# Two megabytes of weight loads under way in place of one, from the fourth pair on, in a fused attention and expert kernel

## The chip, the cores and the metric

The kernel runs on one core of a Trainium2 chip. The metric is the device time of one execution in microseconds (us), lower is better. The core has five engines with an instruction queue each: TensorE (PE; its loading of stationary operands is shown as PEld), VectorE (DVE), ScalarE (ACT), GpSimd (POOL) and SyncE (SP), which here issues nearly all DMA transfers. Each queue runs in its own order; between queues, semaphores decide.

## What is computed

A linear attention with decay over 2 x 8 heads, 768 positions in blocks of 64, then two dense layers with a leaky ReLU between, then two more with a softmax-like gate and a normalisation. The attention output, turned to 1536 tokens x 512, is the input of the rest. The weights are 64-bit floats in memory.

```python
for b in range(nb):                       # 12 blocks of 64 positions
    intra = einsum('bhic,bhjc->bhij', qb, kb) * Dmask
    intra = einsum('bhij,bhjd->bhid', intra, vb)
    inter = einsum('bhid,bhde->bhie', qb * lam_pow, kv_state)
    out[:, :, sl] = intra + inter
    kv_state = lam_block * kv_state + einsum('bhsd,bhse->bhde', kb * rev_pow, vb)
h = x @ w_in                              # 1536x512 @ 512x2048
x = maximum(0.01 * h, h) @ w_out          # 2048x512
h = x @ w_in2                             # 512x1024
solu = h * softmax(h)
ln = (solu - mean) / sqrt(var + 1e-06) * g_ln
return ln @ w_out2                        # 1024x512
```

## The kernel before

The weights of the first two layers come in 17 pairs, counted from 0. Pair n has two halves of 128 x 1024 32-bit words (512 KB): block n of w_in and block n-1 of w_out (pair 0 has the first only, pair 16 the second only). `load_weights(n)` issues the halves from SP. A pair is then turned from 64-bit floats into two matmul operands, a high and a low piece: ACT reads both words (`words`, that is L350 and L354), DVE clamps, shifts and joins them (L360, L370, L379), ACT copies the high piece (`high`, L409), DVE subtracts it for the low piece (`low`, L428). Each pair must have landed before ACT's L350 of it.

The main loop runs over 48 items (3 blocks of 512 tokens, 16 blocks of the hidden layer). For item i, PE runs `l1_mm` of the item (12 matmuls, L439, into one of two `hps` banks), at some items a `step` of the attention (the chunks from 4 on, 8 of them), and `l2_mm` of the item before (12 matmuls, L456, into `acc`). ACT and DVE make the input of `l2_mm` in `l1_split`: prelu (L442) and `ghi` (L445) on ACT, `glo` (L447) on DVE. While the first 16 items run, the pairs are converted ahead of them: at item i, `high` and `low` of pair i+1, the clamp, shift and join of pair i+2, `words` of pair i+3, and `load_weights` of pair i+5. The order on each engine is the order in which the code is written; an instruction that waits holds up all behind it. In ACT's queue, `words` of pair i+3 stands ahead of `high` and of `l1_split` of the next item. At a step, DVE also evicts the scores (`scores_ev`, L204), which frees the `hps` bank for the item after.

All loads go through `load` (L113 to L125). It keeps a list of the loads so far with their sizes, adds up sizes from the newest back, and where the sum with the new load goes over `limit`, the new load waits for that older load to land. `AHEAD` is 2 MB (4 halves, the new one counted), `CALM` is 1 MB (2 halves). The four chunks of attention that are loaded first, the small loads and the later chunks (`load_qk`, `load_kv`, `fix`) have the default `AHEAD`; the weights of L332 have `CALM`, the second half of pair 1 half of it, and pair 0 `AHEAD`. After pair 7, SP issues kv (four loads of 128 KB), `fix` (68 KB) and qk (512 KB), and then pair 8. From chunk 4 on, a kv load also waits until PE and ACT have read the kv of the chunk before, since there is one buffer. `load_weights` of kind "b" (w_out2) uses the same line.

Of the kernel before, what the change touches and what calls it, by code (L numbers as in the profile page):

```python
# [10 lines left out]
U32 = mybir.dt.uint32  # L11
# [13 lines left out]
AHEAD, CALM = 1 << 21, 1 << 20  # L25
# [3 lines left out]
NF = FF1 // P  # L29
# [15 lines left out]
def fused_kernel(ctx: ExitStack, tc: tile.TileContext, att, vt, tab, cst, w_in, w_out, w_in2, w_out2, out):  # L45
# [7 lines left out]
    pe, dve, act, pool, sync = nc.tensor, nc.vector, nc.scalar, nc.gpsimd, nc.sync  # L53
# [59 lines left out]
    def load(queue, out, in_, limit=AHEAD):  # L113

        size = 4
        for n in out.shape:
            size *= n
        ins = queue.dma_start(out=out, in_=in_).ins
        ahead = size
        for before, n in reversed(flight):  # L120
            ahead += n
            if ahead > limit:
                tc.add_manual_dep(ins, before.name, SYNC, reason="bytes under way")
                break
        flight.append((ins, size))  # L125
# [186 lines left out]
    def whole(n):  # L312

        return IN if n == 0 else OUT if n == NF else BOTH

    def load_weights(n, halves=None):
        if n >= len(order):
            return
        kind, f = order[n]
        if n not in raws:  # L320
            if n == NF:
                raws[n] = tmp.tile([P, 1, 512, 2], U32, tag="s", name="rawl")
            else:
                raws[n] = wp.tile([P, 2, 512, 2], U32, tag="w", name="raww")
        t = raws[n]
        if kind == "a":
            load(sync, out=t.rearrange("p h a b -> p (h a b)"), in_=w_in2[f].bitcast(U32))
            return
        halves = halves or whole(n)
        for i in range(halves.start, halves.stop):  # L330
            src = w_out2[f + i] if kind == "b" else w_out[f - 1] if i else w_in[f]
            load(sync, out=t[:, 0 if n == NF else i].rearrange("p a b -> p (a b)"), in_=src.bitcast(U32), limit=(CALM // 2 if n == 1 and i else CALM) if n else AHEAD)  # L332

    def of(n, halves):

# [262 lines left out]
    scan(dfirst, 0, None)  # L598
    load_step(0)
    load_weights(0)  # L600
    load_step(1)
    load_step(2)
    load_step(3)
    load_weights(1, IN)
    load_weights(1, OUT)
    load_weights(2)
    load_weights(3)
# [264 lines left out]
```

## Time and profile before

| | us |
|---|---|
| median of 3 runs | 447.06 (445.94 to 447.09) |
| the profiled execution | 445.46 |
| its span, first to last instruction | 443.70 |
| PE busy | 98% of the span |
| DVE busy | 60% |
| ACT busy | 44% |
| granted clock of TensorE | 1.00 throughout |

In the 40 slices of the page, PE is at nine tenths or more nearly everywhere. DVE is as full from about 10 to 110 us, while the pairs are converted, and the DMA engines move 230 to 300 GB/s in that time and little later. The rows that matter stand further down. In a timeline row, the first number is the start, the second the time until the end of the last of the merged instructions, and the bracket at the end says how long the engine had idled before it and what ended that. A row of a DMA issue gives the size and the time from issue to landing.

### The profile page before, as it was taken

Reading aid. Unit: us, or ns where it says so; the run is one execution under the profiler, and the core shown is the slowest. Engines: PE = TensorE matmul, PEld = TensorE weight load, DVE = VectorE, ACT = ScalarE, POOL = GpSimd, SP = SyncE. Lnnn points to the kernel's source line nnn. Section 1 sums busy time; section 2 is a strip of 40 time slices with the busy share of each in tenths; the row PEclk is TensorE's granted clock in tenths of the full one; section 3 lists DMA queues with packets and bytes.
Section 4 is the critical chain, followed back from the end, with each engine's and each line's share of the span. In section 5 each row is a group of like instructions: output and inputs, shape, how many; then the busy total and the mean of one; then the engine's idle time right before and its main releaser. Section 6 shows DMA issues by size and latency. Waiting matters only on the chain.

```text
span 443.7 us, 8024 instructions
## 1 busy us (share of the span) xinstructions
PE 433.7 (98%) x3270; PEld 356.8 (80%) x3272; DVE 267.3 (60%) x423; ACT 195.6 (44%) x332; POOL 32.0 (7%) x38
## 2 busy tenths in 40 slices
PE   8899998999999999999999999999999999999996
PEld 4788777888888888888888888888888888888886
DVE  4898989999541121211133889716779877777640
ACT  4587866977443222222234778512424322222221
POOL 1500102102201020100000000000000000000000
PEclk9999999999999999999999999999999999999999
DMA  8678788883302030100025542000112222222111
GB/s 296 231 255 260 243 246 236 252 235 98 97 11 87 0 98 0 49 1 0 1 95 188 191 189 96 1 1 10 38 37 72 88 75 73 75 72 74 58 47 47
DMA packets 23699, 46.85 MB, mean 106 GB/s; under 512 B 4336, under 2 KB 12016, under 8 KB 23152
## 3 DMA queue, kind: packets, MB, share of 16 engines
q1 hardware_dynamic: 21792, 44.78, 31.4%
q10 hardware_dynamic: 1872, 1.58, 1.3%
q8 instruction: 25, 0.41, 0.4%
q14 instruction: 10, 0.08, 0.1%
HBM read 37.95 MB, written 3.15 MB: 93 GB/s over the span
## 4 chain that ended last, share of the span: by engine, by line
PE 83%; ACT 0%; issue 0%; DVE 0%
PE acc L456 25%; PE hps L439 25%; PE acc L568 15%; PE aps L476 6%; PE hps L476 5%; PE acc L476 4%; PE aps L250 1%; PE aps L264 1%; PE hps L196 0%; PE aps L210 0%; PE aps L536 0%; PE acc L536 0%; ACT osb L571 0%; DVE state L225 0%
## 5 line engine op out<-in xcount | busy, mean ns | idle before, releaser
L439 PE MATMUL hps<-xhi,wio 128*128 128x512 f32 x384 | 102.9, 390 | 2.7 <-DVE r L204 1.2
L447 DVE TENSOR_TENSOR glo<-hps,ghi 128x512 fp32r<-128x512 f32 x48 | 33.1, 689 | 110.9 <-ACT ghi L445 110.7
L456 PE MATMUL acc<-ghi,wio 128*128 128x512 f32 x384 | 96.1, 392 | 0.6 <-ACT ghi L445 0.6
L439 PEld LDWEIGHTS hps<-xhi,wio 128*128 128x128 f32 x384 | 71.8, 188 | 18.3 <-ACT raww L354 1.6
L456 PEld LDWEIGHTS acc<-ghi,wio 128*128 128x128 f32 x384 | 71.4, 188 | 16.1 <-ACT ghi L445 1.0
L442 ACT ACTIVATE hps<-hps 128x512 f32<-128x512 f32 x48 | 28.0, 584 | 104.9 <-PE hps L439 104.9
L568 PE MATMUL acc<-wb,ln 128*128 128x512 f32 (+1 forms) x312 | 67.6, 373 | 0.0
L568 PEld LDWEIGHTS acc<-wb,ln 128*128 128x128 f32 x312 | 55.3, 188 | 10.2
L439 PE MATMUL hps<-xlo,wio 128*128 128x512 f32 x192 | 51.3, 389 | 0.0
L456 PE MATMUL acc<-glo,wio 128*128 128x512 f32 x192 | 51.3, 389 | 0.0
L439 PEld LDWEIGHTS hps<-xlo,wio 128*128 128x128 f32 x192 | 36.0, 188 | 7.5
L456 PEld LDWEIGHTS acc<-glo,wio 128*128 128x128 f32 x192 | 36.0, 188 | 7.5
L350 ACT ACTIVATE x<-raww 128x1024 f32<-128x1024 f32 (+1 forms) x28 | 27.8, 995 | 11.7 <-DMA raww<-in_w_in_dram 6.6
L379 DVE SCALAR_TENSOR_TENSOR x<-x,raww 128x1024 uint32<-128x1024 uint32 (+1 forms) x28 | 32.2, 1152 | 0.1
L370 DVE SCALAR_TENSOR_TENSOR raww<-x,raww 128x1024 uint32<-128x1024 uint32 (+1 forms) x28 | 29.6, 1056 | 3.8 <-ACT raww L354 1.7
L445 ACT CAST ghi<-hps 128x512 fp32r<-128x512 f32 x48 | 28.2, 587 | 1.5
L354 ACT ACTIVATE raww<-raww 128x1024 uint32<-128x1024 uint16 (+1 forms) x28 | 27.9, 998 | 0.0
L509 POOL TENSOR_TENSOR small<-small,nhalf 128x1 f32<-128x1 f32 x12 | 6.6, 549 | 234.5 <-DVE small L508 234.5
L428 DVE TENSOR_TENSOR wio<-x,wio 128x1024 fp32r<-128x1024 f32 (+1 forms) x21 | 22.2, 1057 | 1.5 <-ACT wio L409 1.5
L409 ACT CAST wio<-x 128x1024 fp32r<-128x1024 f32 (+1 forms) x21 | 17.8, 849 | 11.2 <-DVE x L379 11.2
L165 POOL TENSOR_TENSOR qk<-qk,qpow 128x512 f32<-128x512 f32 x8 | 11.6, 1445 | 140.4 <-PE hps L196 109.6
L571 ACT COPY osb<-acc 128x512 f32<-128x512 f32 (+1 forms) x13 | 7.2, 555 | 32.3 <-PE acc L568 19.5
(115 smaller groups left out, 494.6 us busy)
## 6 DMA issues: line engine op xcount, KB each, us to landing
raww<-in_w_out_dram SPq DMA_DIRECT2D x23, 512.0 KB, 4.3
raww<-in_w_in_dram SPq DMA_DIRECT2D x16, 512.0 KB, 4.3
qk<-in_att_dram SPq DMA_DIRECT2D x8, 512.0 KB, 4.6
raww<-in_w_in_dram SPq DMA_DIRECT2D x4, 1024.0 KB, 4.8
lt<-e SPq DMA_DIRECT2D x124, 32.0 KB, 1.8
out_dram<-osb SPq DMA_DIRECT2D x11, 256.0 KB, 2.2
ldw<-in_att_dram SPq DMA_DIRECT2D x7, 384.0 KB, 5.4
kv<-in_att_dram SPq DMA_DIRECT2D x16, 128.0 KB, 3.4
```

Of the source, the lines that this page charges most:

```text
L350: act.activation(x, raw[:, :, 1].bitcast(F32), AF.Copy, scale=HI_SCALE)
L354: act.activation(raw[:, :, 0], raw.bitcast(U16)[:, :, 1], AF.Copy, scale=LO_SCALE)
L370: dve.scalar_tensor_tensor(raw[:, :, 0], x.bitcast(U32), 3, raw[:, :, 0], op0=ALU.logical_shift_left, op1=ALU.bitwise_or)
L379: dve.scalar_tensor_tensor(xu, xu, 0x80000000, raw[:, :, 0], op0=ALU.bitwise_and, op1=ALU.bitwise_or)
L428: dve.tensor_tensor(t[:, 1, halves], x[:, halves], t[:, 0, halves].bitcast(F32), op=ALU.subtract)
L439: pe.matmul(bank, w[:, s, k], x[b][:, k], start=(i == 0), stop=(i == len(terms) - 1))
L442: act.activation(bank, bank, AF.Prelu, alpha=0.01)
L445: act.copy(ghi, bank)
L447: dve.tensor_tensor(glo, bank, ghi.bitcast(F32), op=ALU.subtract)
L456: pe.matmul(acc[m], w[:, s, m], g, start=(f == 0 and first), stop=(f == NF - 1 and last))
L476: pe.matmul(bank, x[b][:, k, o : o + P], w2_t["a", k, half][:, s], start=(i == 0), stop=(i == len(terms) - 1),)
L568: pe.matmul(po[:, 0:n], x[:, k], w2_t["b", k][:, s, cols], start=(i == 0), stop=(i == len(terms) - 1))
```

## The change

One line in `load_weights`: the limit of a half is 1 MB only for the pairs 1 and 2; from pair 3 on, and for the w_out2 loads, it is 2 MB. Pair 1's second half keeps 0.5 MB, pair 0 keeps 2 MB.

```diff
-load(sync, out=..., in_=src.bitcast(U32), limit=(CALM // 2 if n == 1 and i else CALM) if n else AHEAD)
+load(sync, out=..., in_=src.bitcast(U32), limit=CALM // 2 if n == 1 and i else CALM if n in (1, 2) else AHEAD)
```

The instructions of PE, DVE, ACT and POOL stand in the same order with the same waits. Only what SP's loads wait for differs. Each load counts up one of eight semaphores DMAHW0 to DMAHW7 in turn, and a load that follows 8 loads later on the same one also waits for it. At the first place, the second half of pair 2 counts up DMAHW1, and its first half DMAHW0; the halves of pair 3 count up DMAHW2 and DMAHW3, and qk DMAHW4.

SP, from the second half of pair 2 to pair 4, before:

```order
L118 DMA raww<-in_w_out_dram 128x1024 [waits DMAHW7_49,DMAHW1_49]
L118 DMA raww<-in_w_in_dram 128x1024 [waits DMAHW2_49,DMAHW0_49]
L118 DMA raww<-in_w_out_dram 128x1024 [waits DMAHW3_49,DMAHW1_49]
L118 DMA qk<-in_att_dram 128x2x512
L118 DMA raww<-in_w_in_dram 128x1024 [waits DMAHW5_49,DMAHW3_49]
L118 DMA raww<-in_w_out_dram 128x1024 [waits DMAHW4_49]
```

The same rows of SP after the change:

```order
L118 DMA raww<-in_w_out_dram 128x1024 [waits DMAHW7_49,DMAHW1_49]
L118 DMA raww<-in_w_in_dram 128x1024 [waits DMAHW2_49]
L118 DMA raww<-in_w_out_dram 128x1024 [waits DMAHW3_49]
L118 DMA qk<-in_att_dram 128x2x512 [waits DMAHW0_49]
L118 DMA raww<-in_w_in_dram 128x1024 [waits DMAHW5_49,DMAHW1_49]
L118 DMA raww<-in_w_out_dram 128x1024 [waits DMAHW2_49]
```

The halves of pair 3 no longer wait for pair 2; qk waits for the first half of pair 2, and pair 4 for the second half of pair 2 and the first of pair 3, which are the fourth load before each.

SP, from the second half of pair 7 over kv, `fix` and qk to pair 8, before (`fix` counts up DMAHW1, qk DMAHW2):

```order
L118 DMA raww<-in_w_out_dram 128x1024 [waits DMAHW2_49]
L118 DMA kv<-in_att_dram 64x2x256 x2
L118 DMA kv<-in_vt_dram 64x512 x2
L118 DMA fix<-in_cst_dram 128x136
L118 DMA qk<-in_att_dram 128x2x512 [waits DMAHW3_49]
L118 DMA raww<-in_w_in_dram 128x1024 [waits PE_49,DMAHW1_49,Activation_49,Pool_49]
L118 DMA raww<-in_w_out_dram 128x1024 [waits DMAHW4_49,DMAHW2_49]
```

The same after the change (the second half of pair 7 counts up DMAHW4, the first kv load DMAHW5):

```order
L118 DMA raww<-in_w_out_dram 128x1024 [waits DMAHW0_49]
L118 DMA kv<-in_att_dram 64x2x256 [waits DMAHW1_49]
L118 DMA kv<-in_att_dram 64x2x256
L118 DMA kv<-in_vt_dram 64x512 x2
L118 DMA fix<-in_cst_dram 128x136 [waits DMAHW2_49]
L118 DMA qk<-in_att_dram 128x2x512 [waits DMAHW3_49]
L118 DMA raww<-in_w_in_dram 128x1024 [waits PE_49,DMAHW4_49,Activation_49,Pool_49]
L118 DMA raww<-in_w_out_dram 128x1024 [waits DMAHW5_49]
```

Pair 8 no longer waits for `fix` and qk to land but for the second half of pair 7 and the first kv load; kv and `fix` in turn now wait for halves of pair 6.

## Rows read from the trace of the kernel before

**Rows 1.** The page, busy us of each engine, share of the span, instructions.

```profile
PE 433.7 (98%) x3270; PEld 356.8 (80%) x3272; DVE 267.3 (60%) x423; ACT 195.6 (44%) x332; POOL 32.0 (7%) x38
```

**Rows 2.** Busy time by stretch: us, PE, PEld, DVE, ACT, POOL, PEclk, DMA share, GB/s.

```profile
23.20:45.30 22.10, 22.05 (x96) 17.94 (x96) 20.12 (x35) 18.70 (x32) 0.00 (x0) 1.00 0.78 248
45.30:71.30 26.00, 23.20 (x244) 18.45 (x245) 23.76 (x27) 20.91 (x28) 3.76 (x2) 1.00 0.82 245
71.30:440.30 369.00, 368.98 (x2420) 306.63 (x2420) 208.69 (x334) 144.38 (x245) 20.75 (x24) 1.00 0.25 78
```

**Rows 3.** Timeline of PE, 45.5 to 72.2 us: start, us, instruction, idle before it.

```profile
45.83 0.97 PE L456 MATMUL acc<-ghi,wio 128*128 128x512 f32 x3 [0.56 <-ACT ghi L445]
...
62.06 1.19 PE L439 MATMUL hps<-xhi,wio 128*128 128x512 f32 x4 [1.03 <-ACT wio L409]
...
71.30 1.15 PE L439 MATMUL hps<-xhi,wio 128*128 128x512 f32 x4 [1.25 <-DVE r L204]
```

**Rows 4.** Timeline of ACT, 41 to 62 us.

```profile
41.99 1.14 ACT L350 ACTIVATE x<-raww 128x1024 f32<-128x1024 f32 x1 [0.99 <-DMA raww<-in_w_out_dram]
...
45.19 0.58 ACT L445 CAST ghi<-hps 128x512 fp32r<-128x512 f32 x1
...
54.88 0.59 ACT L445 CAST ghi<-hps 128x512 fp32r<-128x512 f32 x1
58.92 1.12 ACT L350 ACTIVATE x<-raww 128x1024 f32<-128x1024 f32 x1 [3.45 <-DMA raww<-in_w_out_dram]
...
60.97 1.04 ACT L409 CAST wio<-x 128x1024 fp32r<-128x1024 f32 x1
```

**Rows 5.** Waits of DVE, 20 to 72 us: us in total, times, longest.

```profile
DVE x L360 <- ACT x L350: 2.0, 2, 1.5
DVE raww L370 <- ACT raww L354: 0.9, 3, 0.3
```

**Rows 6.** Timeline of DVE, 60 to 71 us.

```profile
60.08 0.69 DVE L360 TENSOR_SCALAR x<-x 128x1024 f32<-128x1024 f32 x1 [1.47 <-ACT x L350]
...
62.25 1.22 DVE L428 TENSOR_TENSOR wio<-x,wio 128x1024 fp32r<-128x1024 f32 x1
...
67.64 2.31 DVE L428 TENSOR_TENSOR wio<-x,wio 128x1024 fp32r<-128x1024 f32 x1
...
70.48 0.67 DVE L204 TENSOR_TENSOR r<-hps,dmask 128x512 f32<-128x512 f32 x1
```

**Rows 7.** Timeline of SP, second halves of the pairs 2, 5 and 8.

```profile
23.22 0.33 SPq L118 DMA_DIRECT2D raww<-in_w_out_dram  x1
...
37.59 0.33 SPq L118 DMA_DIRECT2D raww<-in_w_out_dram  x1
...
54.59 0.33 SPq L118 DMA_DIRECT2D raww<-in_w_out_dram  x1
```

**Rows 8.** Waits of SP, 53 to 60 us: total, times, longest.

```profile
SPq L118 <- DMA fix<-in_cst_dram: 2.7, 1, 2.7
```

**Rows 9.** DMA issues at 23.22, 37.59, 54.59, 75.35 us: KB, us to landing.

```profile
raww<-in_w_out_dram SPq DMA_DIRECT2D x1, 512.0 KB, 3.9
...
raww<-in_w_out_dram SPq DMA_DIRECT2D x1, 512.0 KB, 4.4
...
raww<-in_w_out_dram SPq DMA_DIRECT2D x1, 512.0 KB, 4.3
...
raww<-in_w_in_dram SPq DMA_DIRECT2D x1, 512.0 KB, 3.3
```

**Rows 10.** Busy time by stretch as in rows 2: loads under 2 MB, under 1 MB.

```profile
4.00:16.00 12.00, 11.14 (x307) 7.86 (x310) 7.99 (x21) 5.11 (x13) 4.22 (x4) 1.00 0.94 356
24.00:68.00 44.00, 42.42 (x330) 34.35 (x329) 39.78 (x56) 35.80 (x55) 2.88 (x2) 1.00 0.80 244
```

**Rows 11.** Groups of DVE by form: busy us, mean ns, idle before.

```profile
L204 DVE TENSOR_TENSOR r<-acc,dfirst 128x512 f32<-128x512 f32 x4 | 2.8, 688 | 2.5 <-PE acc L196 2.5
L204 DVE TENSOR_TENSOR r<-hps,dmask 128x512 f32<-128x512 f32 x7 | 4.8, 688 | 0.7 <-PE hps L196 0.6
```

More of the change, by code (lines that the diff above doesn't have):

```diff
@@ L331, in load_weights @@
             src = w_out2[f + i] if kind == "b" else w_out[f - 1] if i else w_in[f]
-            load(sync, out=t[:, 0 if n == NF else i].rearrange("p a b -> p (a b)"), in_=src.bitcast(U32), limit=(CALM // 2 if n == 1 and i else CALM) if n else AHEAD)
+            load(sync, out=t[:, 0 if n == NF else i].rearrange("p a b -> p (a b)"), in_=src.bitcast(U32), limit=CALM // 2 if n == 1 and i else CALM if n in (1, 2) else AHEAD)
     def of(n, halves):
```

## The prediction

> **What bounds the kernel now.** I read the busy times first, then the idle time before TensorE's (PE's) rows in the timeline, then what each of those three waits hangs on, upstream, and last the queue that issues the loads. PE is busy for 433.7 of 443.7 us [rows 1], so a change can win only where PE still idles. From 71.30 to 440.30 us it is busy 368.98 of 369.00 us; from 23.20 to 45.30 us, 22.05 of 22.10; between them, from 45.30 to 71.30 us, 23.20 of 26.00 [rows 2]. Those 2.80 us are three waits in front of PE's rows: 0.56 us at 45.83 for ScalarE's (ACT's) ghi, 1.03 us at 62.06 for ACT's first piece of a weight pair, 1.25 us at 71.30 for VectorE's (DVE's) L204 [rows 3]. Summed, 2.84 us. Since nothing idles behind 71.30, the end moves by what these three lose, and by no more.
>
> All three lead back to loads. Pairs are counted from 0 as in the code; pair n is the half from w_in and the half from w_out.
>
> First wait: ACT idles 0.99 us until 41.99 for the second half of pair 5 [rows 4], which was issued at 37.59 [rows 7] and took 4.4 us to land [rows 9]: 41.99. Behind that wait in ACT's queue stand the two word readings of pair 5 and the high piece of a half of pair 4, and then the prelu and ghi for which PE waits; that ghi ends at 45.78 [rows 4].
>
> Second wait: ACT idles 3.45 us until 58.92 for pair 8 [rows 4], issued at 54.59 [rows 7], landed 4.3 us later [rows 9]. The high piece of pair 7, which PE wants, stands behind it and ends at 62.01.
>
> Third wait: DVE idles 1.47 us until 60.08 for the same reading of pair 8, and from there runs almost without a gap to the L204 that ends at 71.15 [rows 6]. So this wait too is pair 8's landing, passed on through DVE's row.
>
> Pair 8 is late because SP kept it back: SP waited 2.7 us for the small `fix` load before it [rows 8], since with 1 MB allowed the loads ahead of it had to land first.
>
> **The change, part by part.** It adds no instruction to any compute engine and moves none; it changes which landing a load waits for. Three costs follow.
>
> *Rate of the loads.* From 24 to 68 us, with 1 MB allowed, 244 GB/s were moved at a DMA share of 0.80. From 4 to 16 us, where the attention loads already run with 2 MB, it is 356 GB/s at 0.94 [rows 10]. A load that is alone lands in 3.3 us, one of two under way in 4.4 [rows 9], so at 1 MB the engines stand idle part of the time. For the weights at 2 MB the trace has no row; the bounds are 244 (nothing gained) and 356. I take 356, because that row has the same limit and the same queue; its loads have 384 and 256 KB instead of 512, which should not be in its favour.
>
> *When the pairs land.* Up to pair 2's second half, issued at 23.22 and landed 3.9 us later [rows 7, 9], at 27.1, nothing changes. From there, 7 loads of 512 KB (pairs 3 to 5 and one qk) are due up to pair 5: 3.67 MB, 10.3 us at 356 GB/s, so it lands at 37.4 in place of 41.99. Up to pair 8 it is 15 times 512 KB (pairs 3 to 8, two qk, four kv of 128 KB) and 0.07 MB of fix, 7.93 MB: 22.3 us, so 49.4 in place of 58.92. As a test of this sum, at 244 GB/s it gives 27.1 + 32.5 = 59.6, near the 58.92 that the trace has.
>
> *Buffers.* Pairs 6 to 9 take over tiles of the first four attention chunks, all read before the weights' matmuls begin, and pairs 10 and 11 those of pairs 1 and 3, converted long before their turn comes; so no buffer holds these loads. The next load that one holds is kv of step 5, which waits for PE's step 4 before and after alike; SP now stands there longer, with the pairs 12 and on behind it. That costs nothing: they are released after the same step, and with pairs 8 to 11 already landed they no longer wait for them.
>
> Now the three waits. **First:** without ACT's 0.99 us the ghi ends at 44.79, and PE is ready for it at 45.83 − 0.56 = 45.27: gone, 0.48 us to spare. **Second:** PE, 0.56 us earlier, wants the piece of pair 7 at 62.06 − 1.03 − 0.56 = 60.47. ACT is free at 55.47, the end of the ghi at 54.88 [rows 4]; 3.45 us off its end at 62.01 would be 58.56. It also needs DVE's join of pair 7, which was done by 60.08 − 1.47 = 58.61; with 1.04 us for the piece itself, 59.65 at the latest. Gone. **Third:** PE, now 2.84 us earlier, wants DVE's L204 done by 71.15 − 2.84 = 68.31. From 20 to 72 us DVE waits 2.0 + 0.9 us for ACT's word readings (L350, L354) [rows 5], and nearly all of it when ACT itself came late from a load. Given back, the L204 ends at 68.25, just in time. A reserve stands beside it: the L428 at 67.64 took 2.31 us next to GpSimd's scaling; the one at 62.25 took 1.22 [rows 6], and PE's earlier step moves that scaling against DVE's row. So I count the whole 1.25.
>
> After 71.30 both DVE and PE are earlier by the same 2.8 to 2.9 us, so they stand to each other as before, where PE did not wait again. The loads of the last weights also get 2 MB; PE's 368.98 of 369.00 us hide them in either case.
>
> Sum: 0.56 + 1.03 + 1.25 = 2.84 us. The profiled execution took 445.46 us, of which 443.70 are the span; so 442.62 by its own time. It lies 1.60 us under the median of the three runs, 447.06, so **444.2 us** (−0.64%) is forecast there. A measurement of this kernel tells about 0.3%, or 1.3 us, from no change.
>
> How fast must the loads be? The third wait needs pair 8 earlier by 2.9 us, at 56.0: 7.93 MB in 28.9 us, 274 GB/s. Under that the gain shrinks with the landing.
>
> **Rivals.** *1: more loads under way, but hardly more bytes a second.* Then pair 8 comes little earlier and DVE's row carries that on to PE. For it speaks that the 356 GB/s were moved before the weights' matmuls began and by other shapes; against it the DMA share, 0.80 where 0.94 was reached [rows 10]. Halfway between 244 and the 274 that are needed, at 259 GB/s, pair 8 lands at 27.1 + 30.6 = 57.7, 1.2 us earlier, and 445.8 us result; at 244 it is 447.1. A rule speaks for this rival: the Trainium skill, SBUF — State Buffer, section "Can I just issue two DMAs to hit both halves?", says that transfers issued side by side run on the same 16 engines, and that two at once measured only 6% above one. By that rule the rate would rise from 244 to about 259 GB/s, an estimate from it, and the time would be this rival's. The trace has not yet agreed or disagreed for the weights; at its start, with 2 MB, 356 GB/s speak against the rule.
>
> *2: DVE does not get its time back.* DVE is busy 23.76 of 26.00 us in the stretch of the waits [rows 2]; if its 2.9 us stay for other reasons (ACT late for its own work, GpSimd's scaling beside other instructions), the third wait stays and 0.56 + 1.03 = 1.59 us are won: 445.5.
>
> *3: slower, since heavier traffic stretches DVE's instructions.* DVE's row is nearly full from 24 to 68 us, 39.78 of 44.00 [rows 10]. Its 2.9 us of gaps would have to be used up and 1.3 us more, 4.2 of 39.78, so it decides from a stretch of 11%; at 15% (6.0 us) the time would be 450.2. Against it: an L204 of the same size took 688 ns on average, both among the chunks loaded with 2 MB and later [rows 11].
>
> *4: the change does not reach the waits.* If semaphores or buffers hold the loads and not the limit, 447.1. Against it: before pair 8 SP waited for the landing of a load that no buffer needs [rows 8], and the changed program waits there for older ones.
>
> **How the numbers follow.** Forecast 0.72; rival 1 0.12; rival 2 0.08; rival 3 0.05; rival 4 0.03. Rival 2 lies at the edge of what can be told, so 0.05 of it goes to faster and 0.03 to the same: faster 0.77, same 0.12 + 0.03 + 0.03 = 0.18, slower 0.05. The range reaches from 443.4 (the sum and 0.8 us that the three runs lie apart) to 446.0, which takes in rival 2 and the better half of rival 1; left out are rivals 3 and 4 and the rest of 1, some 0.14, and a little noise.
>
> **What would show it.** Right: between 24 and 50 us clearly over 274 GB/s, and then a stretch with hardly a load; pair 8 landed near 49 us; no idle before ACT's L350 for a load past 41 us; none before PE's rows near 45, 60 and 68 us; PE's seamless run from about 68.5 us. Wrong in the first step if the loads stay near 244 GB/s; in the third wait if PE idles at about 68.5 us for DVE with ACT in time; in the sign if DVE's instructions are longer than in the rows here.

## The result and the profile after

The changed kernel takes 441.82 us (441.67 to 442.88), the kernel before 447.07 beside it: a ratio of 0.9893, 95% interval 0.9870 to 0.9915. That is 5.25 us less where 2.84 were forecast, and below the range of 443.4 to 446.0. The profiled execution took 441.67 us, its span 439.9.

Busy time by stretch, answering to [rows 2] (us, PE, PEld, DVE, ACT, POOL, PEclk, DMA share, GB/s):

```profile
23.20:45.30 22.10, 22.10 (x98) 18.30 (x99) 20.76 (x36) 19.84 (x33) 0.00 (x0) 1.00 0.93 330
45.30:71.30 26.00, 26.00 (x261) 21.40 (x260) 25.54 (x32) 20.68 (x28) 5.18 (x3) 1.00 0.66 230
71.30:440.30 369.00, 365.17 (x2405) 303.43 (x2403) 204.71 (x327) 143.85 (x246) 19.71 (x23) 1.00 0.22 73
```

PE idles no more between 45.30 and 71.30 us; the third row ends behind this shorter execution. The chain that ended last now runs through PE alone here; the three blocks that were late in [rows 3]:

```profile
45.13 2.72 PE acc L456 x12
...
60.04 2.72 PE hps L439 x12
...
67.73 2.72 PE hps L439 x12
```

The timeline of ACT, answering to [rows 4]: the reading of pair 5, the ghi behind it, the reading of pair 8 and the high piece of pair 7. None waits for a load.

```profile
40.76 1.14 ACT L350 ACTIVATE x<-raww 128x1024 f32<-128x1024 f32 x1
...
43.98 0.59 ACT L445 CAST ghi<-hps 128x512 fp32r<-128x512 f32 x1
...
54.22 1.18 ACT L350 ACTIVATE x<-raww 128x1024 f32<-128x1024 f32 x1
...
57.49 1.06 ACT L409 CAST wio<-x 128x1024 fp32r<-128x1024 f32 x1 [1.07 <-DVE x L379]
```

DVE's waits from 20 to 72 us, answering to [rows 5], and its timeline, answering to [rows 6]:

```profile
DVE wio L428 <- ACT wio L409: 0.4, 1, 0.4
DVE xlo L303 <- ACT xhi L299: 0.2, 1, 0.2
```

```profile
57.38 0.69 DVE L360 TENSOR_SCALAR x<-x 128x1024 f32<-128x1024 f32 x1
...
64.68 1.22 DVE L428 TENSOR_TENSOR wio<-x,wio 128x1024 fp32r<-128x1024 f32 x1
...
66.42 0.68 DVE L204 TENSOR_TENSOR r<-hps,dmask 128x512 f32<-128x512 f32 x1
```

GpSimd's scaling of `qk` that stands beside the L428, before and after:

```profile
67.24 1.64 POOL L165 TENSOR_TENSOR qk<-qk,qpow 128x512 f32<-128x512 f32 x1 [15.10 <-PE hps L196]
```

```profile
64.92 2.14 POOL L165 TENSOR_TENSOR qk<-qk,qpow 128x512 f32<-128x512 f32 x1 [13.93 <-PE hps L196]
```

SP's issue of the second halves of the pairs 5 and 8, answering to [rows 7], and their landings (KB, us), answering to [rows 9]:

```profile
32.11 0.33 SPq L118 DMA_DIRECT2D raww<-in_w_out_dram  x1
...
44.37 0.41 SPq L118 DMA_DIRECT2D raww<-in_w_out_dram  x1
```

```profile
raww<-in_w_out_dram SPq DMA_DIRECT2D x1, 512.0 KB, 5.0
...
raww<-in_w_out_dram SPq DMA_DIRECT2D x1, 512.0 KB, 6.1
```

So pair 5 landed at 37.1 and pair 8 at 50.5, where 37.4 and 49.4 were worked out. A single load takes longer than before, 6.1 us in place of 4.3, and yet each comes far earlier. The stretch from 24 to 56 us as in [rows 10], and DVE's L204 as in [rows 11]:

```profile
24.00:56.00 32.00, 32.00 (x169) 26.35 (x168) 30.57 (x46) 28.41 (x43) 1.97 (x1) 1.00 0.97 344
```

```profile
L204 DVE TENSOR_TENSOR r<-hps,dmask 128x512 f32<-128x512 f32 x7 | 4.8, 688 | 0.7 <-PE hps L196 0.6
```

344 GB/s at a DMA share of 0.97, and DVE's instruction is as long as before.

The spans of the two profiled executions differ by 443.7 − 439.9 = 3.8 us. The timeline gives 2.84 us of idle time. The rows shown say where most of the rest lies. From the row behind the first wait to the row behind the second it is 16.23 us before and 14.91 after, 1.32 less where 1.03 us of idle time is shown; from there to the row behind the third, 9.24 and 7.69, 1.55 less where 1.25 is shown. Only 0.13 us lie ahead of the weight matmuls, which begin at 23.09 in place of 23.22. What a pause costs beside its idle time, and the 1.5 us by which the medians lie further apart than the profiles, were the questions for the experiments.

### The profile page after: what moved, and what is told of

The parts are those of the page before. It is cut to its first block, busy times and chain, and to the rows that moved or that the text cites. A ratio compares the mean times of both kernels' runs of the same rounds, so it can differ in the third digit from the quotient of the medians.

```text
span 439.9 us, 8018 instructions
## 1 busy us (share of the span) xinstructions
PE 433.0 (98%) x3270; PEld 357.0 (81%) x3272; DVE 266.0 (60%) x423; ACT 195.8 (45%) x332; POOL 32.4 (7%) x38
## 4 chain that ended last, share of the span: by engine, by line
PE 97%; DMA 2%; issue 1%; ACT 0%
PE acc L456 30%; PE hps L439 30%; PE acc L568 15%; PE aps L476 6%; PE hps L476 5%; PE acc L476 4%; PE aps L250 2%; PE aps L264 1%; DMA ldw<-in_att_dram 1%; PE acc L196 1%; DMA tabs<-in_tab_dram 1%; PE aps L210 1%; PE acc L264 1%; PE acc L250 0%; PE aps L582 0%
## 5 line engine op out<-in xcount | busy, mean ns | idle before, releaser
L428 DVE TENSOR_TENSOR wio<-x,wio 128x1024 fp32r<-128x1024 f32 (+1 forms) x21 | 21.1, 1003 | 1.6 <-ACT wio L409 1.5
L571 ACT COPY osb<-acc 128x512 f32<-128x512 f32 (+1 forms) x13 | 7.2, 553 | 32.0 <-PE acc L568 19.5
```

The costliest lines, as they stand in the source:

```text
L428: dve.tensor_tensor(t[:, 1, halves], x[:, halves], t[:, 0, halves].bitcast(F32), op=ALU.subtract)
```

## The experiments

Two theories. **A:** the three waits are all there is, but they cost more than the idle time that one profile showed, since their length changes from execution to execution and each pause costs something besides. **B:** some of the gain lies elsewhere, in the start, in the late loads, or in a rate that helps in another way. All edits are to the limit in `load_weights`, shown as the difference to the changed kernel, but for the pauses.

**The kernel before, profiled once more** (before_again).

```diff
-limit=CALM // 2 if n == 1 and i else CALM if n in (1, 2) else AHEAD
+limit=CALM // 2 if n == 1 and i else CALM if n else AHEAD
```

> The kernel before once more, for a second profiled execution. The changed kernel gained 5.25 us by the medians, but the profiled executions lie only 3.8 us apart, and the profile of before lay 1.6 us under its own median. Theory A (before's loads leave PE waits whose length changes from execution to execution): the three waits of PE between 45 and 72 us stand again, with another sum; an execution near 447 us shows 1 to 1.5 us more of idle time before PE's rows there than the 2.84 us of the first profile. Theory B (the rest of the gain lies elsewhere, at the start or the end): the waits sum to 2.8 us again and the difference between executions is found before 23 us or after 430 us.

Median 446.86 us, 445.37 to 448.21 in ten runs (the kernel before beside it: 444.60 to 448.94 in 19). The profiled execution took 448.21. PE's timeline has the same three waits, and the stretch behind the first one a lower granted clock:

```profile
47.42 3.30 PE L456 MATMUL acc<-ghi,wio 128*128 128x512 f32 x8 [2.62 <-ACT ghi L445]
50.52 1.51 PE L456 MATMUL acc<-glo,wio 128*128 128x512 f32 x4
...
64.76 1.20 PE L439 MATMUL hps<-xhi,wio 128*128 128x512 f32 x4 [0.55 <-ACT wio L409]
...
74.01 1.17 PE L439 MATMUL hps<-xhi,wio 128*128 128x512 f32 x4 [1.27 <-DVE r L204]
```

```profile
47.40:50.80 3.40, 3.38 (x9) 2.74 (x10) 2.83 (x5) 2.46 (x3) 0.00 (x0) 0.59 0.80 239
```

The waits sum to 4.44 us, 1.60 more than in the first profile. Behind the one of 2.62 us, eight matmuls took 3.30 us where 2.11 stand in the first profile, and the four behind them 1.51 where 1.07 stand: the granted clock was 0.59 on average in this stretch, so it was mostly at the lower of its two levels, 1.2 GHz. From the start of the first of these rows to the step behind them PE needed 4.54 us (to 51.96), in the first profile 2.95 (45.83 to 48.78), so the clock cost 1.59 us. The weight matmuls began 0.51 us earlier here, at 22.71. 1.60 + 1.59 − 0.51 = 2.68 us, against 448.21 − 445.46 = 2.75: the three parts account for the difference. Theory A holds, with a term that it did not have.

**The change in two parts of the pairs** (from_six, first_only).

```diff
-limit=CALM // 2 if n == 1 and i else CALM if n in (1, 2) else AHEAD
+limit=CALM // 2 if n == 1 and i else CALM if 0 < n < 6 else AHEAD              # from_six
+limit=CALM // 2 if n == 1 and i else AHEAD if n in (0, 3, 4, 5) else CALM      # first_only
```

> 2 MB only from pair 6 on; pairs 3 to 5 stay at 1 MB. Theory A: the first wait (for ghi, behind pair 5's landing at about 42 us) stays, some 0.6 us and what a restart costs, the waits at 60 to 72 us go: 0.6 to 0.9 us slower than the changed kernel, about 442.6. If instead pairs 3 to 5 carry the gain by bringing the whole row of loads forward, then pair 8 still comes late here and 444 or more result.

444.13 us (443.10 to 448.19), ratio 0.9961 (0.9930 to 0.9992): 1.5 us above what theory A gave, and just within the 444 or more of the other case. The profile, of 444.37 us, still bears out theory A's waits: the first alone is left, and it is longer than in the first profile of before, 1.88 us, since pair 5 landed at 43.73 us in place of 41.99; the second and third are gone. But pair 8 came hardly earlier, at 58.33 in place of 58.92 (ACT's row below). PE did not wait for it because it was itself 1.7 us later, behind its first wait. So the waits are not independent terms: a longer first one covers a part of the next two. Three of the ten executions showed a mean granted clock of 0.995 or 0.996, and they were the slowest, 446.41 to 448.19; the other seven end at 444.93.

```profile
47.56 2.11 PE L456 MATMUL acc<-ghi,wio 128*128 128x512 f32 x8 [1.88 <-ACT ghi L445]
```

```profile
58.33 1.15 ACT L350 ACTIVATE x<-raww 128x1024 f32<-128x1024 f32 x1 [1.30 <-DMA raww<-in_w_out_dram]
```

> 2 MB for the pairs 3 to 5 alone, 1 MB again from pair 6 on. Theory A: what counts is when pair 8 lands, and the four or five us that pairs 3 to 5 win are handed on along SP's row; pair 8 then lands near 54 to 56 us where 56 is needed, so nearly the whole gain stands: 441.8 to 442.8. If the second and third wait are caused by what stands just before pair 8 (kv, fix and qk at 1 MB) and not by lateness handed on, they stay: about 445.

441.89 us, ratio 0.9879 (0.9856 to 0.9902): the whole gain with 2 MB for three pairs. SP issued the second half of pair 8 at 49.53 us, in place of 54.59, it landed 4.2 us later, and PE did not wait. SP still waited 2.3 us for `fix` before pair 8 (between the first two rows shown), where [rows 8] have 2.7, and it did no harm. So lateness is handed on along SP's row, and three pairs that come early carry all later ones.

```profile
45.58 0.43 SPq L118 DMA_DIRECT2D qk<-in_att_dram  x1
48.45 0.33 SPq L118 DMA_DIRECT2D raww<-in_w_in_dram  x1
49.53 0.33 SPq L118 DMA_DIRECT2D raww<-in_w_out_dram  x1
```

**Other limits for the pairs 3 to 16** (three_halves, one_half).

```diff
-limit=CALM // 2 if n == 1 and i else CALM if n in (1, 2) else AHEAD
+limit=CALM // 2 if n == 1 and i else CALM if n in (1, 2) else 3 * CALM // 2 if 3 <= n <= NF else AHEAD   # three_halves
+limit=CALM // 2 if n == 1 and i else CALM if n in (1, 2) else CALM // 2 if 3 <= n <= NF else AHEAD       # one_half
```

> 1.5 MB for pairs 3 to 16 (three halves under way), in place of 1 and 2 MB. Theory A: what counts is pair 8 landing before about 56 us, which needs 274 GB/s; with three under way some 300 to 330 GB/s are moved, so the whole gain stands, 441.8 within 0.5 us. If the gain grows with the bytes under way beyond that (another mechanism than the three waits), this lies between the two kernels, 443 to 446.

> 0.5 MB for pairs 3 to 16, each half waits for the one before to land. A lone load landed in 3.3 us, with its issue 3.7: 140 to 150 GB/s, and 7.4 us for a pair that PE uses in 5.44. Theory A: PE waits again and again from pair 4 or 5 to pair 16; 20 to 35 us slower than before, 467 to 482, all of it as idle time before PE's rows between 40 and 150 us. If transfers side by side gave only 6% more than one alone, the rate would be about 230 GB/s and the time near 448.

1.5 MB give 441.87 us, ratio 0.9909 (0.9873 to 0.9945), the whole gain again. 0.5 MB give 472.95 us in a single run, slower by 26, with idle times of PE from 41 to 130 us, the longest of 5.56, as expected. The stretch from 24 to 56 us with 1.5 MB, then with 0.5 MB:

```profile
24.00:56.00 32.00, 32.00 (x169) 26.32 (x168) 30.59 (x46) 28.25 (x43) 1.97 (x1) 1.00 0.93 310
```

```profile
24.00:56.00 32.00, 25.13 (x102) 19.69 (x101) 22.32 (x36) 18.77 (x31) 0.00 (x0) 0.95 0.51 167
```

So 167, 244 [rows 10], 310 and 344 GB/s with 0.5, 1, 1.5 and 2 MB under way (the 244 from 24 to 68 us; from 24 to 56 us the kernel before has 250). At 310 PE no longer waits, and more brings nothing; no run lies between 250 and 310. The rule of the Trainium skill (SBUF — State Buffer, "Can I just issue two DMAs to hit both halves?"), 6% more from two transfers at once, was measured there on two tiles that begin at partitions 0 and 64. It does not carry over to the loads of 512 KB to 128 partitions here: from one under way to two it is 46%, from two to four 41%.

**The late loads alone** (late_only).

```diff
-limit=CALM // 2 if n == 1 and i else CALM if n in (1, 2) else AHEAD
+limit=CALM // 2 if n == 1 and i else CALM if 0 < n <= NF else AHEAD
```

> The other part of the change alone: 2 MB for the loads of w_out2 only, the 17 pairs as before. PE never waited there, so the time of the kernel before, 446.8 to 447.4, ratio 1.000 within its interval. If these loads carry a part of the gain, 1 us or more faster.

446.27 us, ratio 0.9997 (0.9971 to 1.0023): nothing. Its profile thus shows the old waits a third time, in an execution of 448.07 us with the granted clock at 1.00. They sum to 4.75 us, 1.91 more than in the first profile; the weight matmuls also began 0.63 us later, at 23.85, which together is 2.54 of the 2.61 us by which it is slower:

```profile
47.48 2.12 PE L456 MATMUL acc<-ghi,wio 128*128 128x512 f32 x8 [1.60 <-ACT ghi L445]
...
64.61 1.20 PE L439 MATMUL hps<-xhi,wio 128*128 128x512 f32 x4 [1.90 <-ACT wio L409]
...
73.86 1.17 PE L439 MATMUL hps<-xhi,wio 128*128 128x512 f32 x4 [1.25 <-DVE r L204]
```

**The changed kernel once more** (after_again).

> The changed kernel once more, beside the kernel before on the same chip. If before loses a varying time to late loads and the changed kernel has taken those waits away, its executions lie much closer together than those of before (which reached from 444.6 to 448.9 in the last set): within 1.5 us, median 441.5 to 442.5, and no idle time before PE's rows between 24 and 110 us. If the spread comes from elsewhere, it stays.

441.77 us, 441.56 to 442.38 in four runs, while the kernel before reached from 444.57 to 448.65 in 19 beside it. Its profile shows no idle time before PE's rows from 24 us on. Most of the spread went with the waits.

**What a pause of PE costs** (pause_short, pause_long, pause_longer: 17, 25 and 34 copies).

```diff
+            if i in (19, 23, 27, 31):
+                for _ in range(25):
+                    act.copy(tabs[:, 128:256], tabs[:, 0:128])
             l1_split(u, bank)
```

> The changed kernel with 17 small copies more in ACT's queue ahead of the split of the items 19, 23, 27 and 31, which only delay ghi there; the copies are extra work and write to columns that nobody reads. It measures what a short pause of PE costs beside the idle time shown before its row. Copies start some 0.3 us apart, so ghi comes 5.1 to 5.3 us later, of which some 4 are slack: four pauses of 0.5 to 1.5 us. Theory A (a pause costs more than its idle time, as the three waits that vanished: 3.68 us won where 2.84 us were shown): the time grows by the idle time shown and 0.2 to 0.35 us for each pause, the clock stays at 1.00. If the idle time shown is the whole cost, it grows by that alone.

> The same with 25 copies: four pauses of some 3 to 4 us. In the second profile of the kernel before, the 8 matmuls after a wait of 2.62 us took 3.30 us, where 2.11 are usual after a short one, and the mean granted clock of the stretch was 0.93. Theory A with the clock: the time grows by the idle time shown, 0.2 to 0.35 us for each pause, and 1.0 to 1.5 us more for each pause that the clock falls after; the granted clock is under 1.00 in the stretches behind the pauses. Without such a cost of the clock, by the idle time and 0.2 to 0.35 us each.

> The pauses once more, with 34 copies: 25 copies gave two pauses with 0.8 us shown (at the items 19 and 23) at which the span grew by about 1.1 us each, with the clock at 1.00. Nine copies more, 0.31 to 0.33 us each, give pauses of 3.6 to 3.8 us at the same two items and smaller ones or none at the others. Theory A with the clock: behind each long pause the granted clock falls for some us (0.59 stood behind the 2.62 us in the second profile of before) and each costs 1.0 to 1.5 us beside its idle time and the 0.3 us: with two of them 441.8 + 2 x (3.7 + 0.3 + 1.2) = 452, more if the other two items pause too. Without a cost of the clock 449.8.

pause_short took 442.05 us: the slack was larger than assumed, PE did not pause, and it tells nothing. pause_long took 444.26, with two pauses of 0.81 us and not four longer ones, so here too the slack was misjudged. PE's timeline at the first of them, and the same place of after_again:

```profile
144.03 1.07 PE L439 MATMUL hps<-xhi,wio 128*128 128x512 f32 x4
145.91 2.12 PE L456 MATMUL acc<-ghi,wio 128*128 128x512 f32 x8 [0.81 <-ACT ghi L445]
...
148.78 1.07 PE L439 MATMUL hps<-xhi,wio 128*128 128x512 f32 x4
```

```profile
143.64 1.07 PE L439 MATMUL hps<-xhi,wio 128*128 128x512 f32 x4
...
147.26 1.07 PE L439 MATMUL hps<-xhi,wio 128*128 128x512 f32 x4
```

From the first row to the last it is 4.75 us with the pause and 3.62 without: 1.13 us for 0.81 shown. Half of the 0.32 us is that PE's rows overlap when they follow each other (a row of four starts 0.91 us before the next and is 1.07 long), half that the first twelve matmuls after a pause take 0.15 us longer. It is the same 0.3 us that the second and third wait of the kernel before showed (1.32 for 1.03, 1.55 for 1.25). With it, the three waits cost 2.84 + 0.9 = 3.7 us, where the profiles differ by 3.8.

pause_longer took 461.11 us, more than the 452 expected, since all four items paused: 3.77, 3.78, 2.62 and 2.62 us, 12.8 in sum. Three of the rows behind them, and the stretches behind the first and the last:

```profile
148.95 3.22 PE L456 MATMUL acc<-ghi,wio 128*128 128x512 f32 x8 [3.77 <-ACT ghi L445]
...
208.02 3.52 PE L456 MATMUL acc<-ghi,wio 128*128 128x512 f32 x8 [2.62 <-ACT ghi L445]
...
236.35 2.12 PE L456 MATMUL acc<-ghi,wio 128*128 128x512 f32 x8 [2.62 <-ACT ghi L445]
```

```profile
148.90:152.60 3.70, 3.65 (x10) 2.90 (x11) 1.38 (x2) 1.07 (x2) 0.00 (x0) 0.60 0.00 0
236.00:240.00 4.00, 3.65 (x16) 3.01 (x17) 2.02 (x4) 2.63 (x6) 0.00 (x0) 1.00 0.00 0
```

The span is 20.0 us longer than that of after_again: 12.8 of idle time, 4 x 0.32 = 1.3, and 5.9 more. Of these, 0.5 us lie ahead of the first pause. The rest stands behind the three pauses after which the clock fell: the twelve matmuls there took 4.45, 5.18 and 4.27 us where 2.87 stand behind a pause of 0.81, so the clock cost 1.6, 2.3 and 1.4 us. After the fourth, as long as the third, it stayed at 1.00 and the twelve took 2.88 us. Why is open.

**Two tries for a faster version** (one_in_two, all_two).

```diff
-limit=CALM // 2 if n == 1 and i else CALM if n in (1, 2) else AHEAD
+limit=CALM // 2 if n == 1 and i else CALM if n == 2 else AHEAD     # one_in_two
+limit=AHEAD                                                        # all_two
```

> A try for a faster version: besides the change, the first half of pair 1 has 2 MB in place of 1 MB. In the profile of the changed kernel ACT waits 1.4 us for it until 19.2 us, before the first weight matmul at 23.1. If that wait is on the path, 0.5 to 1.2 us faster than the changed kernel, 440.6 to 441.4; if the attention chunks of the start set the time there, the same 441.8 within 0.4.

> 2 MB for all loads, pairs 1 and 2 included. If more under way is always good, as in one_in_two or a little better, 440.5 to 441.4. If the early loads of pairs 1 and 2 hold back the halves that are needed first, nothing is won or up to 1 us lost: 441.8 to 442.8.

By their medians both are slower than the changed kernel, and they scatter: 443.95 us (440.83 to 446.09) and 445.84 (442.19 to 447.15), ratios to the kernel before 0.9912 (0.9877 to 0.9947) and 0.9967 (0.9935 to 0.9998). Four of the ten executions of one_in_two, 440.83 to 441.49, are faster than any of the changed kernel, about as expected; the other six, 443.93 to 446.09, lose more than that. In the profile of all_two PE stops for 2.95 us among the small matmuls of the attention's start, and of one_in_two for 2.40 in the same place, for nothing that a semaphore shows:

```profile
24.50 0.26 PE L210 MATMUL aps<-ldw 64*64 64x64 f32 x1 [2.95 <-issue]
```

```profile
24.25 0.21 PE L210 MATMUL aps<-ldw 64*64 64x64 f32 x1 [2.40 <-issue]
```

In all_two the granted clock fell behind the stop, to 0.60 on average from 24.40 to 28.40 us, and so to 0.92 in the stretch shown; in one_in_two it was 1.00 from 24.20 to 28.40 us:

```profile
23.20:45.30 22.10, 20.80 (x117) 16.98 (x117) 17.79 (x32) 17.15 (x30) 0.00 (x0) 0.92 0.99 346
```

Seven of the ten executions of all_two had a mean granted clock of 0.992 to 0.996 and took 445.37 to 447.15 us; the three at 0.999 or more took 442.19 to 443.90.

What the DMA queues carried: from 18.5 to 21.8 us in the changed kernel, then in all_two from 18.5 to 21.8 and from 21.8 to 24.6 (packets, MB, share; q8 loads instructions):

```profile
q1 hardware_dynamic: 174, 0.61, 50.5%
q8 instruction: 1, 0.02, 1.7%
```

```profile
q1 hardware_dynamic: 346, 1.27, 95.5%
...
q1 hardware_dynamic: 324, 1.03, 95.1%
q8 instruction: 1, 0.02, 2.1%
```

One packet of instructions is loaded before 21.8 us in the changed kernel, between 19.5 and 20.0; in all_two, with the engines at 95%, and in one_in_two, with 84.5% from 18.5 to 21.8 us, it comes between 22.0 and 22.5, and PE goes on some two us behind it. That the packet holds PE's next instructions is guessed from this order in time and not shown. It would fit that 1 MB is worth keeping for pairs 1 and 2, and that it can go from pair 3 on, where a matmul has 512 columns and PE comes to its next instruction more slowly.

## Why the prediction was right in its mechanism and wrong in its size

- **What bounds it:** right. All three waits were those for pairs 5 and 8, and all three went. The late loads gave nothing (late_only) and the start 0.13 us in the profiles, so theory B fell. One reading was off: pair 8 was not late through SP's wait of 2.7 us for `fix` alone, but because the whole row ahead of it was late; in first_only a wait of 2.3 us for `fix` stayed, and the gain came all the same.
- **Rate and landings:** right. 344 GB/s for 356, pair 5 at 37.1 for 37.4, pair 8 at 50.5 for 49.4. The 274 GB/s worked out as needed stand between 250, where PE waits, and 310, where it does not; nearer than that no run tests them. The choice of the start's row, made under the same limit, was sound; rival 1 fell. The 3.3 us for a load that is alone were read from one with another issued 1 us behind it, but in one_half, where each is alone, it is 3.2 to 3.3.
- **The third wait:** right, with the reserve used. The L204 ended at 67.10, earlier than the 68.31 and the 68.25 of the sum. The reserve was needed: since pauses cost more than their idle time, PE came to this place at 67.57 and not at 68.31, and at 68.25 the L204 would have left a wait of some 0.7 us. The L428 of the pair took 1.22 us in place of 2.31. GpSimd's scaling (`qk`) still ran beside it, but it began 0.40 us before the L428 in the first profile and 0.24 us after it here (64.92 against 64.68), and now it was the scaling that took longer, 2.14 us in place of 1.64; that the order decides is argued from these rows and not tested. Rival 2 fell.
- **Rival 3** fell: the L204 takes 688 ns under 344 GB/s too. Rival 4 fell with the result.
- **The sum, 0.56 + 1.03 + 1.25 = 2.84 us:** this is the step that failed, for two reasons. First, "the end moves by what these three lose, and by no more" took the idle time before a row as the whole cost of a wait. A pause costs about 0.3 us more, measured as 1.13 for 0.81; with three of them 0.9 us. Second, the waits of one execution were taken for those of all: the sum was made on an execution 1.60 us under the median and moved to the median unchanged, as if those 1.60 us lay elsewhere and would stay. That execution, 445.46 us, was faster than each of the three runs shown, and of 70 executions of the kernel before that were timed beside the other kernels only 15 were as fast. Two others, of 448.21 and 448.07 us, had 4.44 and 4.75 us of idle time, and in the first the clock fell as well, 1.6 us. The medians lie 1.5 us further apart than the two profiles. Longer waits are what the slower executions show, once with the clock and once with a start 0.6 us later, but none at the median itself was profiled, so the shares of these in the last 1.5 us stay open. The clock can be only a small one: 11 of the 70 executions had a mean granted clock under 0.997.
- **The range** allowed 0.8 us below the sum, for the scatter of three runs. Since what was removed was itself what scattered, the scatter belonged to the gain: the kernel before reached from 443.65 to 448.94 us in 70 executions, the changed one from 441.56 to 442.88 in eight.

## What to carry to other kernels

When a wait for a load is to be removed, look whether the profiled execution is faster than the median. The waits in it may then be shorter than usual, as they were here; sum them in an execution near the median, if one can be profiled, with some 0.3 us for each pause of PE and more if the clock falls behind it. Find the rate at which the last needed load comes in time, and give as many bytes as reach it; here 1.5 MB, or 2 MB for three pairs only, did as well as 2 MB throughout. Where PE runs many small instructions, be wary of filling the DMA engines: here two kernels that loaded more at 20 us lost more by a stop of PE than they won, though the cause of the stop is not shown.

## What was not expected of the hardware

- A pause of 0.81 us before a matmul of 512 columns cost 1.13 us.
- After two idle times of PE of 2.62 us, and after 3.77 and 3.78 us, the granted clock fell to the lower level for part of the following 3 to 5 us (0.59 and 0.60 as the mean of a stretch), which cost from 1.4 to 2.3 us. It fell too after 2.95 us (all_two) and after 3.08, 5.39 and 5.56 us (one_half: 0.65, 0.50 and 0.64 in the 4 us behind them). After 1.88 us (from_six), 1.90 (late_only) and 2.40 (one_in_two) it did not, nor after one other of 2.62 us (pause_longer) and one of 2.77 (one_half).
- Loads of 512 KB, with the smaller ones between them, moved 167, 244, 310 and 344 GB/s with 0.5, 1, 1.5 and 2 MB under way.
- With the DMA engines 95% (all_two) and 84.5% (one_in_two) busy from 18.5 to 21.8 us, a packet of instructions came 2.0 to 3.0 us later than in the changed kernel, and PE stood 2.95 and 2.40 us. That one caused the other is not shown.
